# A conditional region between the halves of a product, and a last copy shared by two engines, in a routed attention and mixture-of-experts kernel

## The chip, the cores and the metric

The kernel runs on one core of one Trainium2 chip. The metric is the device time of one execution in microseconds (us), lower is better. The median of the runs of the kernel before is 705.09 us.

## The reference

The computation is an attention block with clusters, followed by a mixture of experts with one expert per token. What matters here is the second part, with 3072 tokens, 512 features, 8 experts and a hidden width of 1024:

```python
def _moe_ref(x, expert_emb, tau, w1, w2):
    N, D = x.shape
    ...
    logits = xn @ en.T / tau
    expert_idx = np.argmax(logits, axis=1)
    ...
    gate_w = probs[np.arange(N), expert_idx]
    out = np.zeros((N, D), dtype=np.float32)
    for e in range(E):
        mask = expert_idx == e
        if not mask.any():
            continue
        h = np.maximum(x[mask] @ w1[e], 0.0)
        out[mask] = gate_w[mask, None] * (h @ w2[e])
    return out.astype(np.float32)
```

How many tokens an expert gets depends on the data, so the kernel has to be right for every distribution.

## The kernel before

The attention fills about the first half of the time. Behind it the experts' work is a list of items, each for one expert: four early items, eight "sized" items (one per expert, with a fixed number of token slots from 272 down to 160), and eight "block" items of 128 tokens each for what the sized ones don't hold. The list `later` holds the last 16 of these, alternating: its numbers 13, 14 and 15 are a block, the sized item with 160 slots, and the last block. Two weight buffers `w1s` and `w2s` (slots 0 and 1) alternate; blocks 13 and 15 both use slot 1.

The order of the instructions is written out by hand for all engines (`manual_schedule`), so that each engine runs its instructions in the order in which the code issues them. A block goes as follows:

- DVE turns the gathered rows (`turn_x`, L1173).
- PE makes the first product in two halves (`hidden`, L1289); ACT applies the relu to each half into the tile `hT` (L1296).
- PE makes the second product (`result`, L1305): four matmuls that need the first half of `hT` and four that need the second, summed in one bank `y_ps`.
- ACT copies `y_ps` to `y`, scaled by the gate (L1316), and POOL scatters the rows of `y` to the output (L1080).

A sized item goes alike, with `sized_hidden` (L1204, relu at L1211; its results go through four banks in turn, three of `psH` and one of `psX`), `order_w2` (DVE reorders w2, L1189), `sized_result` (L1241, turned back by DVE at L1250 and scaled at L1264) and `send` (scatters, L1080). SP loads the weights (L1119).

If the fixed slots and blocks are not enough, the function `overflow` computes up to 14 further blocks of kind "whole". Its body stands under `tc.If(n_used > KX)` (L1565), where `n_used` is read from the tile `used` by every engine (L1550). With the inputs of the reference the body is not entered. Every engine that has work in the body still loads the register and branches, and on the path past the body it raises its semaphores by what the body would have raised, after waiting for its own work in front of the region (SP also for its weight loads, POOL also for the landing of its gathers and scatters). Work behind the region that depends on another engine waits for these raised values.

In the kernel before, `overflow()` stands at the head of the step for `later[14]`, in front of the weight loads of the last block:

```python
            if i == LAST - 1:
                overflow()
                weights1(later[LAST])
                weights2(later[LAST])
```

Of the kernel before, what the change touches and what calls it, by code (L numbers as in the profile page):

```python
# [9 lines left out]
F32 = mybir.dt.float32  # L10
BF16 = mybir.dt.bfloat16
I32 = mybir.dt.int32
ALU = mybir.AluOpType
ACTF = mybir.ActivationFunctionType
# [4 lines left out]
P = 128  # L19
# [20 lines left out]
def kernel(  # L40
# [12 lines left out]
    nc = tc.nc  # L53
# [3 lines left out]
    E, DM = moe_expert_emb.shape  # L57
    F = moe_w1.shape[2]
# [6 lines left out]
    KF = F // P  # L65
# [7 lines left out]
    CAPS = (272, 256, 240, 224, 208, 192, 176, 160)  # L73
    KX = 8
# [11 lines left out]
    scale = 1.0 / float(D) ** 0.5  # L86
# [80 lines left out]
    def bank(kind, pool):  # L167

        tiles = turns.setdefault(kind, [])
        if len(tiles) < 2:  # L170
            name = f"{kind}{len(tiles)}"
            tiles.append(pool.tile([P, 512], F32, tag=name, name=name))
            return tiles[-1]
        tiles.append(tiles.pop(0))
        return tiles[-1]
# [926 lines left out]
    def expert_of(it):  # L1102
        table = {"early": e_early, "sized": e_sized, "block": e_block, "whole": e_block}[it.kind]
        return nc.values_load(
            table[0:1, it.j : it.j + 1], engines=(EngineType.SP,), min_val=0, max_val=E - 1
        )
# [10 lines left out]
    def load_part(w, x, e, chunks, i, parts):  # L1117
        c = slice(chunks // parts * i, chunks // parts * (i + 1))
        nc.sync.dma_start(  # L1119
            out=w[:, c], in_=x[ds(e, 1)].rearrange("o (c p) f -> p (o c) f", p=P)[:, c]  # L1120
        )
# [108 lines left out]
    def sized_result(it):  # L1230

        d, C, n = mo[it], CAPS[it.j], WIDE[it.j]
        ys = d["ys"] = szp.tile([P, max(WIDE), P], F32, tag="ys", name="ys")
        cut = KF - 2
        bks = {}

        def products(g, fs):
            if g not in bks:
                bks[g] = misc() if g >= 2 else bank("y_ps", psY)
            for f in fs:  # L1240
                nc.tensor.matmul(  # L1241
                    bks[g][:, 0:C],
                    lhsT=d["w2"][:, f, P * g : P * g + P],
                    rhs=d["hT"][:, f, 0:C],
                    start=(f == 0),
                    stop=(f == KF - 1),
                )

        def turn_back(g):
            nc.vector.transpose(  # L1250
                ys[:, 0:n, SQ * g : SQ * g + SQ],
                bks[g][:, 0 : SQ * n].rearrange("p (u t) -> p u t", t=SQ),
            )

        products(0, range(cut))
        products(1, range(cut))
        for g in range(2):
            products(g, range(cut, KF))
            turn_back(g)
        for g in range(2, KD):  # L1260
            products(g, range(KF))
            turn_back(g)
        u0 = FIRST[it.j]
        nc.vector.tensor_tensor(  # L1264
            ys[:, 0:n], ys[:, 0:n], bc(flat(gates4)[:, u0 : u0 + n], [P, n, P], 2), ALU.mult
        )
# [9 lines left out]
    def flat(t):  # L1276
        return t.rearrange("p k w -> p (k w)")

    def hidden(it, halves=(0, 1)):

        d = mo[it]
        for half in halves:
            if half == 0:
                d["hT"] = mop.tile([P, F], F32, tag="hT", name="hT")
            f0 = 512 * half
            bk = psH.tile([P, 512], F32, tag="h_ps", name="h_ps")
            for m in range(0, 512, P):
                for c in range(KD):
                    nc.tensor.matmul(  # L1289
                        bk[:, m : m + P],  # L1290
                        lhsT=w1s[it.slot][:, c, f0 + m : f0 + m + P],
                        rhs=d["xT"][:, P * c : P * c + P],
                        start=(c == 0),
                        stop=(c == KD - 1),
                    )
            nc.scalar.activation(d["hT"][:, f0 : f0 + 512], bk, ACTF.Relu)  # L1296

    def result(it, halves=(0, 1)):
        d = mo[it]
        for half in halves:  # L1300
            if half == 0:
                d["y_ps"] = bank("y_ps", psY)
            bk = d["y_ps"]
            for c in range(KF // 2 * half, KF // 2 * half + KF // 2):
                nc.tensor.matmul(  # L1305
                    bk,
                    lhsT=d["hT"][:, P * c : P * c + P],
                    rhs=w2s[it.slot][:, c],
                    start=(c == 0),
                    stop=(c == KF - 1),  # L1310
                )
            if half == 1:
                to = (sidxs[0] if it.kind == "early" else it.tables[2])[:, it.col : it.col + 1]
                y = mop.tile([P, DM], F32, tag="y", name="y", bufs=3)
                gate = d["gate"] if it.kind == "early" else it.gates[:, it.col : it.col + 1]
                nc.scalar.activation(y, bk, ACTF.Copy, scale=gate)  # L1316
                scatter(out[:], to, y, N)
                del mo[it]

# [30 lines left out]
    later = items[KA:]  # L1350
# [73 lines left out]
    with tc.manual_schedule(engines=by_hand):  # L1424
# [123 lines left out]

        def overflow():
            n_used = nc.values_load(used[0:1, 0:1], min_val=0, max_val=KX + NO)  # L1550
            slot = later[-1].slot

            def more(j0, n):
                for j in range(j0, j0 + n):
                    it = Item("whole", KX + j, slot, more_tables)
                    it.col, it.gates, it.xin = j, more_gates, xin
                    weights1(it)
                    weights2(it)
                    fetch(it)
                    order_x(it)  # L1560
                    turn_x(it, nc.scalar.copy)
                    hidden(it)
                    result(it)

            with tc.If(n_used > KX):  # L1565
                more_tables = [None] + [
                    mop.tile([P, NO], I32, tag=f"more{i}", name=f"more{i}", bufs=1)
                    for i in range(2)
                ]
                xin = szp.tile([P, max(WIDE), P], F32, tag="ys", name="ys")[:, 0:NQ]  # L1570
                pb.hot_blocks(NB, NO)
                pb.tokens(NO)
                pb.token_rows(more_tables[1], more_tables[2])
                more_gates = mop.tile([P, NO], F32, tag="more_gates", name="more_gates", bufs=1)
                pb.hot_gates(NO)
                pb.gates(more_gates)
                more(0, MORE[0])
                with tc.If(n_used > KX + MORE[0]):
                    more(MORE[0], MORE[1])
                    with tc.If(n_used > KX + MORE[0] + MORE[1]):  # L1580
                        more(MORE[0] + MORE[1], MORE[2])

        LAST = len(later) - 1
        for i, it in enumerate(later):
            if i == LAST - 1:
                overflow()
                weights1(later[LAST])
                weights2(later[LAST])
            if it.kind == "sized":
                order_w2(it)  # L1590
            if i + 1 < len(later):
                turn_x(later[i + 1])
            if i > 0 and i + 2 < len(later) and later[i + 2].kind == "sized":
                fetch(later[i + 2])
            if i > 0 and later[i - 1].kind == "sized":
                send(later[i - 1])
                if i == LAST:
                    nc.gpsimd.drain()
            if it.kind == "sized":
                sized_hidden(it)  # L1600
            else:
                hidden(it)
            if i == 0:
                pb.gates(slot_gates)
            for j in range(i + 2, min(i + 4, len(later))):
                if later[j].kind == "block" and later[j] not in mo:
                    if it.kind == "sized":
                        nc.gpsimd.tensor_copy(pace, mo[it]["hT"][0:1, KF - 1, 0:1])
                        fetch(later[j])
            if i + 2 < LAST:  # L1610
                weights1(later[i + 2])
                if it.kind == "sized":
                    weights2(later[i + 2])
            if it.kind == "sized":
                sized_result(it)
            else:
                result(it)
            if i == 0:
                fetch(later[2])
                spread_gates()  # L1620
            if i + 2 < LAST and it.kind != "sized":
                weights2(later[i + 2])
# [45 lines left out]
```

## Time and profile before

| | |
|---|---|
| runs of the kernel before | 704.33, 706.35, 704.28, 705.85 us; median 705.09 |
| the profiled execution | 706.03 us, span from first to last instruction 704.2 us |
| granted TensorE clock | 0.999 |
| PE busy | 688.3 us (98% of the span) |
| DVE, ACT, POOL busy | 385.7, 262.8, 252.4 us |
| PE's last matmul starts / span ends | 697.9 / 704.2 us |

How to read what follows: times in a view are microseconds from the start of the span. PE is the matrix engine and PEld its weight loads, which overlap the matmuls; DVE, ACT and POOL are the vector, scalar and GpSimd engines; SP issues DMA. A name with a q (PEldq, ACTq) is the engine's instruction queue, with its branches and semaphore instructions, which are not counted as busy. An fp32 matmul leaves two records. Matmuls are pipelined, so that one record may last 0.59 us while the next starts 0.43 us after it; their ends are modelled. In brackets stands the idle time of an engine ahead of an instruction and what ended it; "remote" is a releaser that the trace does not name.

### The profile page before, as it was taken

How to read it: one execution, taken by the hardware profiler on the slowest of the kernel's cores; microseconds unless marked ns; L12 is line 12 of the kernel's file. 1: busy time of each engine (PE TensorE's matmuls, PEld its weight loads, DVE VectorE, ACT ScalarE, POOL GpSimd, SP SyncE). 2: the span in 40 equal slices, each digit the busy share in tenths (PEclk: the TensorE clock that was granted, in tenths of full speed). 3: DMA queues.
4: the chain of work that ended last, by engine and by line, in shares of the span. 5: the costliest groups of instructions: out<-in, count | busy, mean ns of one | idle time of the engine just before them, and what ended most of it. 6: DMA issues, size and time to landing. Idle time of an engine off the chain costs nothing.

```text
span 704.2 us, 16130 instructions
## 1 busy us (share of the span) xinstructions
PE 688.3 (98%) x6517; PEld 460.9 (65%) x6517; DVE 385.7 (55%) x666; ACT 262.8 (37%) x444; POOL 252.4 (36%) x403
## 2 busy tenths in 40 slices
PE   8999999999999999999999999999999999999896
PEld 3544444444444444455866678887979797979694
DVE  5878988998989999999573121240311203030210
ACT  5556565577656765576224110101010111111111
POOL 2122221321122221263215356646363554545402
PEclk9999999999999999999999999999999999999999
DMA  9765667785887578688799967358768585969360
GB/s 139 98 99 101 100 95 98 148 141 106 105 141 150 97 154 157 170 254 252 195 308 361 336 237 280 100 204 290 258 237 306 180 314 218 317 229 332 117 240 32
DMA packets 244156, 135.55 MB, mean 192 GB/s; under 512 B 207840, under 2 KB 207842, under 8 KB 244076
## 3 DMA queue, kind: packets, MB, share of 16 engines
q1 hardware_dynamic: 237084, 121.08, 65.4%
q0 software_dynamic: 6016, 13.12, 5.2%
q8 instruction: 54, 0.88, 0.5%
q10 hardware_dynamic: 976, 0.25, 0.2%
q14 instruction: 26, 0.21, 0.1%
HBM read 115.92 MB, written 13.12 MB: 183 GB/s over the span
## 4 chain that ended last, share of the span: by engine, by line
PE 75%; DVE 8%; issue 6%; DMA 6%; SPq 1%; ACT 1%; POOL 1%; another core or an unknown queue 1%; POOLq 0%; DVEq 0%; ACTq 0%
PE s_ps L512 16%; PE o_ps L534 12%; PE h_ps L1289 10%; PE y_ps L1305 9%; PE h_ps L1204 9%; PE misc L1241 5%; PE y_ps L1241 5%; DVE acc L553 4%; DMA out_dram<-ys,spidx 3%; PE x_ps L1204 3%; PE misc L581 2%; PE misc L405 1%; SPq L212 1%; DMA q<-in_q_dram 1%
## 5 line engine op out<-in xcount | busy, mean ns | idle before, releaser
L523 ACT ACTIVATE prob<-s_ps 128x768 f32<-128x768 f32 x192 | 154.2, 813 | 105.4 <-PE s_ps L512 104.4
L512 PE MATMUL s_ps<-qT,kT 64*64 64x384 f32 x1536 | 156.1, 482 | 0.0
L534 PE MATMUL o_ps<-prob,v 64*64 64x385 f32 x1536 | 142.1, 484 | 0.0
L553 DVE TENSOR_TENSOR acc<-acc,prob 128x768 f32<-128x768 f32 x128 | 127.3, 995 | 8.8 <-ACT prob L523 0.5
L534 PEld LDWEIGHTS o_ps<-prob,v 64*64 64x64 f32 x1536 | 59.3, 133 | 64.2 <-issue 56.3
L1250 DVE STREAM_TRANSPOSE ys<-y_ps 128x256 f32<-128x256 f32 (+4 forms) x16 | 6.5, 413 | 155.5 <-PE y_ps L1241 139.4
L1289 PE MATMUL h_ps<-xTm,w1s 128*128 128x128 f32 x768 | 88.8, 275 | 1.5 <-issue 1.5
L1289 PEld LDWEIGHTS h_ps<-xTm,w1s 128*128 128x128 f32 x768 | 87.5, 192 | 3.2 <-issue 2.8
L567 POOL TENSOR_TENSOR o_sum<-o_sb 128x385 f32<-128x385 f32 x30 | 29.9, 998 | 162.3 <-ACT o_sb L558 162.3
L1305 PE MATMUL y_ps<-w2s,hT 128*128 128x512 f32 x192 | 85.3, 594 | 1.7 <-ACT hT L1296 1.0
L1080 POOL DMA_INDIRECT out_dram<-ys,spidx x56 | 57.0, 1018 | 74.0 <-DVE ys L1264 59.4
L512 PEld LDWEIGHTS s_ps<-qT,kT 64*64 64x64 f32 x1536 | 56.1, 133 | 36.3 <-issue 32.2
L1296 ACT ACTIVATE hT<-h_ps 128x512 f32<-128x512 f32 x24 | 14.3, 596 | 163.0 <-PE h_ps L1289 119.0
L1204 PE MATMUL h_ps<-xTs,w1s 128*128 128x272 f32 (+7 forms) x384 | 72.9, 346 | 1.3 <-ACTq L1565 1.3
L1204 PEld LDWEIGHTS h_ps<-xTs,w1s 128*128 128x128 f32 x384 | 66.6, 190 | 8.1 <-issue 2.4
L512 PE MATMUL s_ps<-hot 64*64 64x384 bf16 x768 | 65.1, 325 | 1.9 <-ACT prob L523 0.7
L1305 PEld LDWEIGHTS y_ps<-w2s,hT 128*128 128x128 f32 x192 | 35.3, 190 | 42.9 <-issue 40.3
L1069 POOL DMA_INDIRECT xs<-x_rows,gpidx x56 | 56.4, 1008 | 17.1 <-issue 17.1
L512 PEld LDWEIGHTS <-hot 64*64 64x64 bf16 x768 | 24.3, 106 | 45.3 <-issue 41.9
L602 POOL COPY inv<-inv 32x12 f32<-32x12 f32 x120 | 31.2, 260 | 50.7 <-DVE inv L599 46.3
L1241 PE MATMUL misc<-hTs,w2o 128*128 128x272 f32 (+7 forms) x256 | 48.0, 346 | 0.0
L1241 PE MATMUL y_ps<-hTs,w2o 128*128 128x272 f32 (+7 forms) x256 | 48.0, 346 | 0.0
(270 smaller groups left out, 688.6 us busy)
## 6 DMA issues: line engine op xcount, KB each, us to landing
w1s<-in_moe_w_dram SPq DMA_DIRECT2D x18, 2048.0 KB
w2s<-in_moe_w_dram SPq DMA_DIRECT2D x18, 2048.0 KB
v<-in_v_dram SPq DMA_DIRECT2D x128, 48.0 KB
k<-in_k_dram SPq DMA_DIRECT2D x62, 96.0 KB
q<-in_q_dram SPq DMA_DIRECT2D x60, 96.0 KB
x_rows<-xb SPq DMA_DIRECT2D x60, 96.0 KB
xr<-x_rows SPq DMA_DIRECT2D x9, 512.0 KB
w1s<-in_moe_w_dram SPq DMA_DIRECT2D x4, 1024.0 KB
```

Source lines behind the costliest of these rows:

```text
L512: nc.tensor.matmul(s_ps[D * half : D * half + D, h, 0:HS], lhsT=l[rows, half], rhs=r[rows], start=part == (1 if len(parts) < 2 else 0), st ...
L523: nc.scalar.activation(d["prob"][:, :, 0:HS], d["s_ps"][:, :, 0:HS], ACTF.Exp, scale=scale)
L534: nc.tensor.matmul(g["o_ps"][D * h : D * h + D, half, 0:HE], lhsT=ld[n]["v"][keys, j, h], rhs=d["prob"][keys, h, 0:HE], start=(j == 0), st ...
L553: nc.vector.tensor_tensor(g["acc"], g["acc"], d["prob"][:, :, 0:HS], ALU.add)
L567: add(t["o_sum"][:, hq], t["o_sb"][:, 0], t["o_sb"][:, 1], ALU.add)
L602: nc.gpsimd.tensor_copy(inv2[M * to : M * to + M, :, i % 2], inv[M * i : M * i + M])
L1069: nc.gpsimd.indirect_dma_start(out=to, out_offset=None, in_=of, in_offset=bass.IndirectOffsetOnAxis(ap=at, axis=0), bounds_check=n - 1, oo ...
L1080: inst = nc.gpsimd.indirect_dma_start(out=to, out_offset=bass.IndirectOffsetOnAxis(ap=at, axis=0), in_=of, in_offset=None, bounds_check=n - 1,
L1204: nc.tensor.matmul(bk, lhsT=w1s[it.slot][:, c, P * f : P * f + P], rhs=d["xT"][:, c, 0:C], start=(c == 0), stop=(c == KD - 1),)
L1241: nc.tensor.matmul(bks[g][:, 0:C], lhsT=d["w2"][:, f, P * g : P * g + P], rhs=d["hT"][:, f, 0:C], start=(f == 0), stop=(f == KF - 1),)
L1289: nc.tensor.matmul(bk[:, m : m + P], lhsT=w1s[it.slot][:, c, f0 + m : f0 + m + P], rhs=d["xT"][:, P * c : P * c + P], start=(c == 0), stop ...
L1305: nc.tensor.matmul(bk, lhsT=d["hT"][:, P * c : P * c + P], rhs=w2s[it.slot][:, c], start=(c == 0), stop=(c == KF - 1),)
```

## The change

Two parts. First, `overflow()` moves in the code from the head of the step for `later[14]` to the middle of the second product of `later[13]`: behind the four matmuls of its first half and in front of the four of its second half, and so also in front of that block's copy of `y` and its scatter. For this the items of the region get other tiles: `hT` is taken from the sized items' tile `hTs`, `y_ps` from the pool `psH`, and their weights go to the slot of `later[13]`. At the end of the region's body the second half of that block's `w2` is loaded again. Second, for the last block alone the copy of `y_ps` to `y` is made by ACT for columns 0 to 255 and by DVE for columns 256 to 511.

```diff
@@ hidden @@
             if half == 0:
-                d["hT"] = mop.tile([P, F], F32, tag="hT", name="hT")
+                d["hT"] = (
+                    flat(szp.tile([P, KF, max(CAPS)], F32, tag="hTs", name="hTs", bufs=1))[:, 0:F]
+                    if it.kind == "whole"
+                    else mop.tile([P, F], F32, tag="hT", name="hT")
+                )
@@ result @@
             if half == 0:
-                d["y_ps"] = bank("y_ps", psY)
+                d["y_ps"] = (
+                    psH.tile([P, 512], F32, tag="h_ps", name="h_ps")
+                    if it.kind == "whole"
+                    else bank("y_ps", psY)
+                )
@@ result @@
                 gate = d["gate"] if it.kind == "early" else it.gates[:, it.col : it.col + 1]
-                nc.scalar.activation(y, bk, ACTF.Copy, scale=gate)
+                h = DM // 2 if it is later[-1] else DM
+                nc.scalar.activation(y[:, 0:h], bk[:, 0:h], ACTF.Copy, scale=gate)
+                if h < DM:
+                    nc.vector.tensor_scalar(y[:, h:DM], bk[:, h:DM], gate, None, ALU.mult)
                 scatter(out[:], to, y, N)
@@ overflow @@
-            slot = later[-1].slot
+            own = later[-3]
...
-                    it = Item("whole", KX + j, slot, more_tables)
+                    it = Item("whole", KX + j, own.slot, more_tables)
...
                     with tc.If(n_used > KX + MORE[0] + MORE[1]):
                         more(MORE[0] + MORE[1], MORE[2])
+                own.e = expert_of(own)
+                load_part(w2s[own.slot], moe_w2, own.e, KF, 1, 2)
@@ the loop over later @@
             if i == LAST - 1:
-                overflow()
                 weights1(later[LAST])
                 weights2(later[LAST])
...
             if it.kind == "sized":
                 sized_result(it)
+            elif i == LAST - 2:
+                result(it, (0,))
+                overflow()
+                result(it, (1,))
             else:
                 result(it)
```

## The prediction

> **What bounds the kernel now.** I read the page first: the share of PE, then the slices.
>
> ```profile
> PE 688.3 (98%) x6517; PEld 460.9 (65%) x6517; DVE 385.7 (55%) x666; ACT 262.8 (37%) x444; POOL 252.4 (36%) x403
> ```
>
> PE fills 98% of a span of 704.2 us, and the other engines have slack. So an edit is worth what it does to a gap of PE, or to the tail after PE's last instruction. Both edits lie in the last 50 us, so I went to the timeline of PE there.
>
> ```profile
> 650.67 7.31 PE L1289 MATMUL h_ps<-xTm,w1s 128*128 128x128 f32 x64
> 657.81 3.60 PE L1305 MATMUL y_ps<-w2s,hT 128*128 128x512 f32 x8
> 661.92 3.70 PE L1305 MATMUL y_ps<-w2s,hT 128*128 128x512 f32 x8 [0.51 <-ACT hT L1296]
> 666.89 3.50 PE L1204 MATMUL h_ps<-xTs,w1s 128*128 128x160 f32 x24 [1.27 <-ACTq L1565]
> ...
> 684.35 7.31 PE L1289 MATMUL h_ps<-xTm,w1s 128*128 128x128 f32 x64
> 691.49 7.03 PE L1305 MATMUL y_ps<-w2s,hT 128*128 128x512 f32 x16
> ```
>
> The columns are start, duration, engine and line, with the idle time before it and its releaser in brackets. The second product of the block before the last sized item is two pieces of 8 records (4 matmuls of two records each). Between them PE waits 0.51 us for the second half of hT. After them it waits 1.27 us for the conditional region at L1565. From 666.89 to 698.52 there is no further gap. So at most 1.8 us can be won in front of the last 32 us, and the rest is the tail. The timeline of ACT shows what else stands at these two places:
>
> ```profile
> 661.27 0.60 ACT L1296 ACTIVATE hT<-h_ps 128x512 f32<-128x512 f32 x1 [6.23 <-remote]
> 665.66 0.69 ACT L1316 ACTIVATE y<-y_ps,slot_gates 128x512 f32<-128x512 f32 x1 [3.79 <-PE y_ps L1305]
> ...
> 698.56 0.69 ACT L1316 ACTIVATE y<-y_ps,slot_gates 128x512 f32<-128x512 f32 x1 [4.68 <-PE y_ps L1305]
> ```
>
> Why the gap is 1.27 us is read from the region's own line:
>
> ```profile
> L1565 PEldq COMPARE_BRANCH  x1: 3837/3837/3837, 662.6 to 662.6; - x1
> L1565 ACTq COMPARE_BRANCH  x1: 45/45/45, 666.2 to 666.2; - x1
> L1565 PEldq EVENT_SEMAPHORE  x1: 51/51/51, 666.5 to 666.5; - x1
> L1565 ACTq EVENT_SEMAPHORE  x1: 17/17/17, 666.6 to 666.6; - x1
> L1565 POOLq COMPARE_BRANCH  x1: 45/45/45, 667.0 to 667.0; - x1
> L1565 POOLq INC_SWDGE_SEM  x1: 1230/1230/1230, 674.0 to 674.0; - x1
> ```
>
> PE's branch lasts 3.84 us, from 662.63 to 666.47, while its array works until 665.62; 0.85 us of it stick out. ACT branches only after its copy of y, and PE waits for the semaphore that ACT raises in the region (666.6). Both meet at 666.89.
>
> **The region (part one).** In the built program PE now issues 4 of the 8 matmuls, the region, then the other 4 and the sized item. Nothing is computed more or less when the region is not entered.
>
> PE's branch. PE's queue runs ahead of its array: the wait in front of y's first matmul was read at 655.8 and that matmul ran at 657.81, 2 us or 17 records later. The 8 records of the first half enter as slots come free, one per 0.11 us (7.31 us / 64), so the load of `used` is reached at about 656.8. Load to branch took 0.7 us (661.9 to 662.6), so the branch starts near 657.5 and ends near 661.3, at the duration of the row. The first half ends at 661.41. Then comes PE's wait on its own semaphore, one wait on weight queues (SP's part of the region ended at 656.9), and the matmul: in the trace the way from the branch's end to the matmul was 0.39 us with one wait more. That gives 661.8. The other condition, the second half of hT, comes at 661.87 as before ("remote" means that the trace does not name what released it, so I keep its time). I take a start of the second half at 662.0 in place of 661.92. Bounds: 661.45 if both are early (no gap at all); 662.65 if the branch can only finish once the array has drained, as it did 0.85 us after the drain in the trace (661.41 + 0.85 + 0.39).
>
> What follows. Eight records from 661.92 put the next one at 665.46 (the last of eight starts at 665.03, spacing 0.43), and the sized item started at 666.89. Now it stands directly behind, its ACT condition raised in the region: ACT branches after hT, not after y. ACT's load, branch and semaphore took 0.97 us from the start of the instruction before, so they are done at 662.25. The sized item starts at 662.0 + 3.54 = 665.54, **1.35 us earlier**; at the bounds 1.9 and 0.7 us. Its operands wait long: xTs was turned at 653.1 and w2o copied at 659.4.
>
> What is queued behind. ACT: y of this block now follows the region and also waits for the software-queue semaphores that POOL raises there; behind y stand the eight copies of hTs, and PE has four banks for them. POOL: its region now stands in front of this block's scatter, and waits for the scatters before it. The last of these six was made from 659.11 to 660.23; the DMA share falls to zero in the stretch after 661, so it landed about 661.5. Three semaphores (0.26 us) and the increment (1.23 us) follow: 663.0, 2.5 us before ACT needs it at 665.5. The scatter itself moves from 666.62 by at most a microsecond, and POOL had 18.45 us of idle before its next. SP: the load of the last block's w1s waits for PE's region, 666.5 in the trace and about 661.8 now; its w2s follows at 665.6 instead of 667.3. Both are used at 683 or later, so nothing changes. The additional reload of half of w2s lies inside the branch that is not taken. DVE's turn of xTm (666.68, released by ACT's region) goes to 662.3 and had 17 us of slack.
>
> **The last copy (part two).** One ACT copy of 512 columns (0.687 us) becomes ACT on 256 and DVE on 256. In the built program DVE does not wait for PE but for ACT's half, and POOL waits only for DVE. So they run one after the other. ACT with 256: the relu took 0.597 us on 512 and 0.30 on 160, 0.84 ns per column, so 0.687 - 0.213 = 0.47 us. DVE with 256 out of PSUM: turns of 128x256 took 0.44 us, a copy of 128x200 took 0.367; I take 0.42. The hop from ACT to DVE: 0.05 us (666.63 to 666.68). Sum 0.94 in place of 0.69: **0.25 us later**; bounds 0.4 later, and 0.2 earlier if both halves ran side by side. POOL's scatter follows 0.28 us after either engine, and the 0.97 us of the scatter and the end after it stay.
>
> The page PSUM — Partial Sum Buffer of the Trainium skill, in the section on PSUM bank collisions, says that two engines must not touch one bank and quadrant at once, readers included. That speaks against the halves, and would be why the program orders them; no run shown here has two readers in one bank. By that rule the sum is 0.25 us later; by the bare rows of the two halves side by side it would be 0.2 us earlier.
>
> The page Advanced Engine Details and Errata, section Control Flow Timing, gives about 108 ns for a compare-and-branch; the row on PE has 3837 ns. The page Runtime: NRT & Kernel Launch, section Instruction fetch mechanics, has a reason: a taken branch beyond the loaded window has to fetch its page first. By 108 ns the sum stays as it is and the first rival below goes; by the row the branch needs nearly all of the first half's 3.6 us.
>
> **Sum.** -1.35 + 0.25 = -1.1 us. The profiled execution took 706.03 us with a span of 704.2, so it becomes 704.9 with a span of 703.1. It stands at the slow end of its four runs (704.28 to 706.35); on their median of 705.09 it is **704.0 us**. A change under 0.3% (2.1 us) is about what a measurement of this kernel can't tell from none, and this lies under it. The bounds give -1.9 - 0.2 = -2.1 and -0.7 + 0.4 = -0.3.
>
> **Rivals.** *The branch is not covered (slower).* If PE loads `used` only when the first half has left the array (661.4), or its fetch queues behind another one, the 3.84 us stand bare: the branch ends at 661.41 + 0.7 + 3.84 = 665.9, the second half starts at 666.3, the sized item at 669.9, 3.0 us later than now, 3.2 with the tail: 708.3 us. Half of that exposed is +1.1 us, 706.2. It turns from gain to loss when the branch ends after about 662.7 (start of the second half 663.1, the sized item at 666.64, plus the tail's 0.25). For: the cover has only 0.1 us to spare. Against: the branches of ACT and POOL (45 ns) ran while their engines were busy, and PE's load came within 0.02 us of the first of four matmuls that were still to run. Chance 0.18.
>
> *POOL holds ACT (slower).* If POOL's region ends near 675.2, as it did before, ACT's y goes from 665.66 to 675.2, and hTs behind it to 676; PE fills its four banks until about 670 and then stands 6 us: 705.09 - 1.1 + 6 = 710. It decides from an end after about 669. Against: in the trace that region waited for the scatter issued at 666.62, and this one is no longer ahead of it. Chance 0.06.
>
> *Side by side.* Both halves of the copy overlap: -1.35 - 0.2 = -1.55 us, 703.5 us. Against: the order of waits in the program. Chance 0.08.
>
> **How the numbers follow.** The forecast has 0.68. Its four runs before spread over 2 us, so a true -1.1 reads as more than 2.1 us faster in about one of five (0.15 of it, with 0.05 from the side-by-side rival: 0.20). Slower by over 2.1 us: more than half of the uncovered branch (0.10) and POOL's hold (0.05): 0.15. The rest is 0.65. The range goes from -2.4 (the lower bound and a little spread), 702.7, to half of the uncovered branch with spread, 706.7; beyond it lie the fully bare branch and POOL's hold.
>
> **What would show it.** Right: a gap of 0.5 to 0.7 us between the two pieces of 8 records, none in front of L1204 behind them; PE's branch starting at 657 to 658; POOL's increment over by 663; at the end ACT's half, then DVE's, then the scatter, 0.94 us in all. Wrong: a gap over 1.7 us between the halves (the branch is bare), ACT's y later than 666 with PE idle in the sized item (POOL holds it), or a changed time with these stretches unchanged.

## The result and the profile after

The changed kernel takes 704.44 us (median), against 705.76 us for the kernel before on the same chip: a ratio of 0.9983, 95% interval 0.9977 to 0.9989, or 1.2 us faster; predicted were 704.0 us from 705.09, or 1.1 us faster. The profiled execution has a span of 702.5 us (704.2 before) at a granted clock of 0.999.

PE's timeline, to be held against the four lines of before around 657.81:

```profile
650.25 7.31 PE L1293 MATMUL h_ps<-xTm,w1s 128*128 128x128 f32 x64
657.40 3.60 PE L1313 MATMUL y_ps<-w2s,hT 128*128 128x512 f32 x8
661.53 3.70 PE L1313 MATMUL y_ps<-w2s,hT 128*128 128x512 f32 x8 [0.53 <-ACT hT L1300]
665.07 3.42 PE L1204 MATMUL h_ps<-xTs,w1s 128*128 128x160 f32 x24
...
689.60 7.03 PE L1313 MATMUL y_ps<-w2s,hT 128*128 128x512 f32 x16
```

The gap of 0.5 us between the halves, which ACT's `hT` releases, is still there. The gap of 1.27 us in front of the sized item (L1204) is gone. From the first matmul of the second product to the first of the sized item it was 666.89 - 657.81 = 9.08 us; now it is 665.07 - 657.40 = 7.67 us. I call this stretch *the stage*; it has shrunk by 1.41 us.

The region's own line (now L1576), as in the prediction:

```profile
L1576 PEldq COMPARE_BRANCH  x1: 3332/3332/3332, 656.9 to 656.9; - x1
L1576 PEldq EVENT_SEMAPHORE  x1: 51/51/51, 661.0 to 661.0; - x1
L1576 POOLq INC_SWDGE_SEM  x1: 1210/1210/1210, 661.4 to 661.4; - x1
...
L1576 ACTq EVENT_SEMAPHORE  x1: 17/17/17, 661.9 to 661.9; - x1
```

PE's branch runs from 656.90 to 660.23 and lies wholly beside the first half, which leaves the array at 661.00. PE's semaphore instruction (661.04) stands directly behind that end: it is PE's wait for its own work. What holds the second half after that is `hT`, from ACT's timeline:

```profile
660.88 0.60 ACT L1300 ACTIVATE hT<-h_ps 128x512 f32<-128x512 f32 x1 [6.26 <-remote]
```

It ends at 661.48 and the matmul starts at 661.53. At the end of the kernel the timeline of all engines shows the two halves of the copy and the scatter:

```profile
696.72 0.47 ACT L1325 ACTIVATE y<-y_ps,slot_gates 128x256 f32<-128x256 f32 x1 [4.73 <-PE y_ps L1313]
697.23 0.48 DVE L1327 TENSOR_SCALAR y<-y_ps,slot_gates 128x256 f32<-128x256 f32 x1 [13.36 <-ACT y L1325]
697.98 0.97 POOL L1080 DMA_INDIRECT out_dram<-y,sidx  x1 [7.78 <-DVE y L1327]
```

DVE waits for ACT, not for PE. PE's last product ends at 696.63, so 1.35 us pass until the scatter starts; before it was 699.53 - 698.52 = 1.01 us.

The account of the spans: the stage -1.41, from the sized item to PE's last end -0.07 (31.63 to 31.56), the tail behind PE +0.19 (5.68 to 5.87, the longer copy less a slightly shorter end). That is -1.29 us, and the medians differ by 1.32; single executions of either kernel scatter by some 5 us, so that two traces and two medians come this close is partly chance. The spans differ by 0.41 us more, because the first half of the second product starts 0.41 us earlier in this execution, ahead of the place that was changed.

### The profile page after: what moved, and what is told of

Read it like the earlier page. It is cut to its first block, busy times and chain, and to the rows that moved or that the text cites. A ratio compares the mean times of both kernels' runs of the same rounds, so it can differ in the third digit from the quotient of the medians.

```text
span 702.5 us, 16133 instructions
## 1 busy us (share of the span) xinstructions
PE 687.1 (98%) x6517; PEld 460.9 (66%) x6517; DVE 386.5 (55%) x667; ACT 262.8 (37%) x444; POOL 252.3 (36%) x403
## 4 chain that ended last, share of the span: by engine, by line
PE 76%; issue 8%; DVE 7%; DMA 3%; POOL 2%; ACT 1%; another core or an unknown queue 1%; SPq 0%; POOLq 0%; DVEq 0%; ACTq 0%
PE s_ps L512 16%; PE o_ps L534 13%; PE h_ps L1293 10%; PE y_ps L1313 9%; PE h_ps L1204 9%; PE misc L1241 5%; PE y_ps L1241 5%; PE x_ps L1204 3%; DVE acc L553 3%; PE misc L581 2%; DMA q<-in_q_dram 2%; PE misc L405 1%; DMA out_dram<-ys,spidx 1%; PE misc L660 1%
## 5 line engine op out<-in xcount | busy, mean ns | idle before, releaser
L1204 PE MATMUL h_ps<-xTs,w1s 128*128 128x272 f32 (+7 forms) x384 | 72.8, 346 | 0.0
L1204 PEld LDWEIGHTS h_ps<-xTs,w1s 128*128 128x128 f32 x384 | 66.7, 190 | 6.5 <-issue 2.9
```

Source lines behind the costliest of these rows:

```text
L1204: nc.tensor.matmul(bk, lhsT=w1s[it.slot][:, c, P * f : P * f + P], rhs=d["xT"][:, c, 0:C], start=(c == 0), stop=(c == KD - 1),)
```

## Experiments

Theory before these runs: the region costs PE time only through the gap around it, the move takes that gap from 1.27 us to almost nothing, and the halved copy gives a quarter of it back. The rival is that PE's branch of 3.3 to 3.8 us is what the place decides about, and that the new place only just covers it.

The kernels ran in three sets, each on one chip of its own with runs of the kernel before beside it (701.33, 703.59 and 706.06 us). The stage, measured in every trace:

| kernel (set) | stage, us | gap between the halves + gap in front of the sized item |
|---|---|---|
| before | 9.08 | 0.51 + 1.27 |
| after | 7.67 | 0.53 + 0 |
| old place, halved copy (1) | 8.11 | 0 + 1.08 |
| new place, one copy (1) | 7.41 | 0.30 + 0 |
| new place, two banks, ACT and DVE (1) | 7.41 | 0.30 + 0 |
| no region (1) | 6.87 | 0 + 0 |
| the change again (2) | 7.52 | 0.38 + 0 |
| old place, short body (2) | 7.33 | 0 + 0.30 |
| region in front of the product (2) | 10.00 | 0 + 0, and 3.52 in front of the product |
| new place, two banks, ACT (2) | 7.49 | 0.37 + 0 |
| old place, tiles of its own (3) | 8.83 | 0.45 + 1.08 |
| new place, shared bank (3) | 8.09 | 0.95 + 0 |
| region in front of the copy (3) | 8.73 | 0.54 + 0.90 |
| region in front of the copy, two banks, ACT (3) | 9.01 | 0.53 + 1.18 |

**The parts alone.** The region at its new place with one ACT copy at the end:

```diff
-                h = DM // 2 if it is later[-1] else DM
-                nc.scalar.activation(y[:, 0:h], bk[:, 0:h], ACTF.Copy, scale=gate)
-                if h < DM:
-                    nc.vector.tensor_scalar(y[:, h:DM], bk[:, h:DM], gate, None, ALU.mult)
+                nc.scalar.activation(y, bk, ACTF.Copy, scale=gate)
```

> The region in its new place with its own tiles; the last block's result copied by ACT alone, as in the kernel before. Theory (the place gives the gain, the halved copy costs): the gap in front of L1204 goes from 1.27 us to 0, the sized item follows its predecessor 1.43 us sooner; from PE's last matmul to the end of y 0.72 us, as before; 1.4 us faster than before (ratio 0.9980) and 0.36 us faster than the change as made. Rival (the halved copy carries part of the gain): slower than the change as made, 0.9 us or less faster than before.

And the halved copy in the kernel before:

```diff
-                nc.scalar.activation(y, bk, ACTF.Copy, scale=gate)
+                h = DM // 2 if it is later[-1] else DM
+                nc.scalar.activation(y[:, 0:h], bk[:, 0:h], ACTF.Copy, scale=gate)
+                if h < DM:
+                    nc.vector.tensor_scalar(y[:, h:DM], bk[:, h:DM], gate, None, ALU.mult)
```

> The region in its old place; only the last block's copy in two halves. Theory: ACT's half 0.47 us, then DVE's half 0.48 us, 1.08 us from PE's last matmul to the end of y instead of 0.72; the gap of 1.27 us stays; 0.36 us slower than before (ratio 1.0005). Rival (halves help): 0.2 us or more faster.

Measured: the region alone 0.9993 (0.9984 to 1.0002), 0.5 us faster; the halves alone 1.0005 (0.9996 to 1.0014), 0.35 us slower, with 1.31 us from PE's end to the scatter. Neither interval leaves out 1. The region brought less than the stage of the first two traces says, and PE's timeline of the region alone shows why:

```profile
654.13 3.60 PE L1313 MATMUL y_ps<-w2s,hT 128*128 128x512 f32 x8
658.03 3.67 PE L1313 MATMUL y_ps<-w2s,hT 128*128 128x512 f32 x8 [0.30 <-PEq L1573]
661.54 3.42 PE L1204 MATMUL h_ps<-xTs,w1s 128*128 128x160 f32 x24
```

```profile
L1573 PEldq COMPARE_BRANCH  x1: 3712/3712/3712, 653.6 to 653.6; - x1
L1573 PEldq EVENT_SEMAPHORE  x1: 51/51/51, 657.8 to 657.8; - x1
```

```profile
654.33 0.60 ACT L1300 ACTIVATE hT<-h_ps 128x512 f32<-128x512 f32 x1 [2.98 <-PE h_ps L1293]
```

Here the second half is not released by `hT` but by PE's own queue in the region, after 0.30 us. PE's branch was over at 657.34, still under the first half, which left the array at 657.73; only then does PE's wait for its own work end. ACT's relu followed the first product at once in all four traces of this set; in the traces of before and after it started over 3 us later than that. With `hT` on time the old place has no gap between the halves, and in front of the sized item (timeline, then the region's line, of the halves alone):

```profile
662.18 3.53 PE L1204 MATMUL h_ps<-xTs,w1s 128*128 128x160 f32 x24 [1.08 <-ACTq L1568]
```

```profile
L1568 PEldq COMPARE_BRANCH  x1: 3388/3388/3388, 655.5 to 655.5; - x1
L1568 PEldq EVENT_SEMAPHORE  x1: 51/51/51, 661.1 to 661.1; - x1
L1568 ACTq COMPARE_BRANCH  x1: 45/45/45, 661.7 to 661.7; - x1
L1568 ACTq EVENT_SEMAPHORE  x1: 17/17/17, 662.1 to 662.1; - x1
```

PE's branch was over at 658.9, 2.2 us before the product left the array. ACT came last: it branches only behind its copy of `y`. So on this chip the old place costs 1.08 us through ACT, the new one 0.30 us through PE's wait for an empty array, and the move gains 0.70 us of stage, not 1.41. The move alone was not run on a chip with a late `hT`.

**No region at all**, one copy at the end (the overflow blocks are left out of the computation):

```diff
                 result(it, (0,))
-                overflow()
                 result(it, (1,))
```

> As the region alone, but without the call of the region (the overflow blocks, which these inputs do not use, are left out). Theory (the moved region costs nothing any more): the gap between the halves of the second product stays at 0.5 us, since it is hT's, and there is none behind; same time as the region alone within 0.2 us. Rival (the branch is what holds the second half): the gap between the halves shrinks to 0.1 us or less, 0.4 us faster than the region alone.

Measured: 0.9966 (0.9952 to 0.998), 2.4 us faster than before. Its stage is 0.54 us shorter than with the region at the new place, and the gap between the halves is gone:

```profile
653.69 7.03 PE L1313 MATMUL y_ps<-w2s,hT 128*128 128x512 f32 x16
660.56 3.42 PE L1204 MATMUL h_ps<-xTs,w1s 128*128 128x160 f32 x24
```

So the expectation's theory, that the moved region costs nothing, is wrong where `hT` is on time. The rival's size fits, but not its reason: the region holds the second half by PE's wait for its empty array, when the branch is already over. A further 0.67 us comes from the end: the scatter's start to the end of the span takes 3.88 us in place of 4.55, and SP goes through 6 final semaphores there in place of 10. Against the region alone that accounts for 1.2 of 1.9 us (0.9966 against 0.9993); the stage also starts 0.44 us earlier in this trace, which nothing here explains. So with `hT` on time a better place could give at most 0.54 us of stage.

**Where the price of PE's branch comes from.** The region in front of the whole second product:

```diff
-                result(it, (0,))
-                overflow()
-                result(it, (1,))
+                overflow()
+                result(it)
...
-                load_part(w2s[own.slot], moe_w2, own.e, KF, 1, 2)
+                weights2(own)
```

> The region moved alone (one ACT copy at the end), but to the place between the first and the second product of the same block, in front of all 16 matmuls of the second product. Theory 'length': PE's taken branch lasts 3.3 to 3.8 us whatever the array does, starting about 1.4 us before the first product leaves the array, because PE's queue reads some 17 short matmuls ahead; so it ends 1.9 to 2.4 us after that, 0.3 us of semaphores follow, and the gap between the two products is 2.2 to 2.7 us with none later: 1.1 to 1.6 us slower than the kernel before where that one has a gap of 1.08 us in front of the sized item, 0.4 to 0.9 us slower where it has 0.5 + 1.27 us. Rival 'drain': the branch itself costs little (45 ns as on ACT) and only lasts until the array is empty; then the gap is 0.3 us and the kernel 0.8 us faster than before.

Measured: 1.0056 (1.004 to 1.0071), 3.9 us slower. The direction is that of "length" and against "drain", but the size was missed. PE's timeline, the stretches around it (the column behind the busy times is the granted clock), and the branch:

```profile
659.20 10.16 PE L1313 MATMUL y_ps<-w2s,hT 128*128 128x512 f32 x16 [3.52 <-PEq L1573]
669.20 3.42 PE L1204 MATMUL h_ps<-xTs,w1s 128*128 128x160 f32 x24
```

```profile
655.70:659.20 3.50, 0.00 (x1) 0.03 (x1) 0.78 (x3) 0.37 (x1) 1.93 (x2) 0.90 0.17 50
659.20:664.00 4.80, 4.80 (x6) 2.15 (x7) 0.71 (x1) 0.23 (x1) 0.00 (x0) 0.50 0.84 282
```

```profile
L1573 PEldq COMPARE_BRANCH  x1: 3452/3452/3452, 654.1 to 654.1; - x1
L1573 PEldq EVENT_SEMAPHORE  x1: 51/51/51, 658.8 to 658.8; - x1
```

```profile
658.83 0.60 ACT L1300 ACTIVATE hT<-h_ps 128x512 f32<-128x512 f32 x1 [6.10 <-remote]
```

The branch ends at 657.6, 1.9 us after the first product left the array at 655.67, as foreseen. Two things were not. PE's own wait in the region ended only at 658.83, together with ACT's late relu, so the gap is 3.52 us. And the granted clock fell to 0.50, near 658.5 and so still inside the gap, and stayed there for the first seven of the product's sixteen records (two to a matmul), which stand 0.85 us apart in place of 0.43: 10.16 us in place of 7.03. The gap cost its length and 3.1 us more.

The record has two more long gaps of PE. They stand near 400 us in the two kernels further down with the region in front of the copy, where PE waits for `w2s`, 2.54 us in the one and 3.53 us in the other. Both times the product behind took 8.80 us, and 7.11 in the trace of before. In the first of them (the second view is of the stretches before, in and after the slow part):

```profile
402.36 8.80 PE L1313 MATMUL y_ps<-w2s,hT 128*128 128x512 f32 x16 [2.54 <-DMA w2s<-in_moe_w_dram]
```

```profile
402.30:403.30 1.00, 0.94 (x3) 0.49 (x4) 0.00 (x0) 0.00 (x0) 0.00 (x0) 1.00 1.06 412
403.40:406.70 3.30, 3.30 (x6) 1.24 (x5) 0.00 (x0) 0.00 (x0) 0.00 (x0) 0.50 1.06 398
406.80:411.00 4.20, 4.20 (x11) 1.62 (x9) 0.00 (x0) 0.00 (x0) 0.00 (x0) 1.00 1.03 411
```

The clock fell 1 us after the matmuls had begun again. No gap of 1.27 us or less lowered it in any trace. The Trainium skill, TensorE: Matmul & The Clock Gate, section "What's actually happening", says that an idle window of about 3.4 us sends the array back to half its clock. The gap of 3.52 us would fit that; the one of 2.54 us is shorter and did it too, so by the measurement less idle time is enough.

The other test of the price is the kernel before with a short body, so that the jump is near; it also takes ACT's semaphore out of the region:

```diff
-                more(0, MORE[0])
-                with tc.If(n_used > KX + MORE[0]):
-                    more(MORE[0], MORE[1])
-                    with tc.If(n_used > KX + MORE[0] + MORE[1]):
-                        more(MORE[0] + MORE[1], MORE[2])
```

> The kernel before with the region at its old place, but without the overflow blocks in its body (it then computes nothing for a seventh and further block of a crowded expert list; with these inputs the region is not entered). ACT has nothing left in the region and neither branches nor raises a semaphore; PE's and DVE's parts stay, with a shorter jump. Theory 'ACT's turn': the old gap in front of the sized item is ACT's, which loads, branches and signals only after its copy of y; without it the gap falls from about 1.1 to 0.3-0.4 us (PE's own wait until its array is empty, and its semaphores), 0.7 us faster than before or more. Rival 'PE's branch': PE's branch sticks out; its row stays at 3.3 us or more, ends after the array, and the gap stays near 1.1 us. If the jump's distance makes the price, the row falls under 1 us.

Measured: 0.9981 (0.9972 to 0.999), 1.3 us faster at the old place. The region's line and PE's timeline:

```profile
L1565 PEldq COMPARE_BRANCH  x1: 236/236/236, 659.3 to 659.3; - x1
```

```profile
663.51 3.50 PE L1204 MATMUL h_ps<-xTs,w1s 128*128 128x160 f32 x24 [0.30 <-PEq L1565]
```

PE's branch takes 0.24 us in place of 3.3 to 3.8. The size of the body that is jumped over sets the price here, and the array's state does not. The Trainium skill, Runtime: NRT & Kernel Launch, section Instruction fetch mechanics, says that a taken branch to a target outside the loaded window has to fetch that page first; this pair of rows agrees. In the stretch of each of the twelve long branches the DMA view has one packet on the instruction queue q8, and in that of the short one none. The kernel does two things at once, though: PE's long branch and its wait for ACT are both gone, so it does not tell which of them made the old gap. (ACT still branches here, against the expectation, but only at 663.78, when the sized item has started.)

**Which of the two made the old gap.** The region between the whole second product (16 records) and the copy of its result: PE meets it at the old place, ACT one copy earlier.

```diff
-                result(it, (0,))
-                overflow()
-                result(it, (1,))
+                result(it, (0, 1))     # the matmuls
+                overflow()
+                result(it, (2,))       # the copy and the scatter
```

> Region between all 16 matmuls of the second product and the copy of their result (one ACT copy at the end). PE meets it at the old place, its jump as far as before; ACT meets it before its copy of y in place of behind it. Theory 'ACT's turn': ACT's branch and signal are long over when the product ends, PE's branch of 3.3 to 3.8 us lies under the product where that is not held up, and what is left is PE's own wait for its empty array: a gap of 0.3 us in front of the sized item, 7.33 us from the product's first matmul to the sized item's (7.41 to 7.52 with the region between the halves): 0.8 us faster than before, 0.1 to 0.2 us faster than the region between the halves. Rival 'PE's branch': PE meets the region where it did, so the gap stays at 1.1 us or more.

This kernel also loses the copies and scatters of the first two early blocks, which ask for their halves by number, and near 400 us it has the gap of 2.54 us and the slow product shown above. So its total (1.0009, 0.9994 to 1.0024) can't be read; the stage can. PE's timeline and the region's line:

```profile
663.20 3.70 PE L1313 MATMUL y_ps<-w2s,hT 128*128 128x512 f32 x8 [0.54 <-ACT hT L1300]
667.79 3.50 PE L1204 MATMUL h_ps<-xTs,w1s 128*128 128x160 f32 x24 [0.90 <-ACT y L1324]
```

```profile
L1573 ACTq EVENT_SEMAPHORE  x1: 17/17/17, 663.5 to 663.5; - x1
L1573 PEldq COMPARE_BRANCH  x1: 3568/3568/3568, 663.8 to 663.8; - x1
```

ACT's turn can't be the whole of it. ACT had signalled at 663.56, yet the gap is 0.90 us: PE's branch lasted until 667.37, while the product left the array at 666.90. (The view names ACT's copy of `y`, which ended 0.12 us ahead of the matmul; the last kernel of this section, with the same place and a branch 0.28 us longer, has a gap 0.28 us longer and names PE's queue.) On this chip `hT` was late again (a gap of 0.54 us between the halves), and that is the link. While the second half waits for `hT`, PE's queue stands at that wait and can't read ahead to the region: here the branch starts 0.66 us after the relu's end, and 0.66 to 0.76 us after it in all five traces with the region behind a late `hT`, while with `hT` on time (the halves alone) it started 1.5 us after the product's first matmul. The late branch then outlasts the half's 3.7 us. So the old place has two limits close together. With `hT` on time, PE reads ahead and ACT's turn remains (1.08). With `hT` late, the branch sticks out as well (0.85 us in the trace of before, 0.90 of gap here without ACT). The new place avoids both, since the queue meets no wait on `hT`'s second half in front of the region.

The trace of before can now be read more closely than its view does. Where ACT comes last (the halves alone, and the tiles alone below), the sized item starts 0.05 us behind ACT's semaphore. Where PE's branch comes last (here and in the last kernel of this section), it starts 0.31 us behind PE's. In the trace of before it started 0.24 us behind ACT's (666.65) and 0.31 us behind PE's (666.58). The view names ACT, but by these distances PE's branch ended that gap of 1.27 us; ACT's turn alone would have ended it 0.2 us sooner, at the same 1.08 us.

**The tiles.** The kernel before with the other tiles for the region's items alone (the first two hunks of the change):

> The kernel before with the tiles of its own alone, the region at its old place. Theory: no change (within 0.3 us), and the gap of 1.1 us or more in front of the sized item is still there, released by ACT's region. Rival: the tiles loosen PE's wait in front of the sized item; then the gap falls to 0.3-0.4 us, as in the kernel with the short region, 0.7 us faster.

Measured: 1.0003 (0.9988 to 1.0019), with 0.45 + 1.08 us of gaps and the branch from 663.16 to 666.77:

```profile
667.33 3.53 PE L1204 MATMUL h_ps<-xTs,w1s 128*128 128x160 f32 x24 [1.08 <-ACTq L1573]
```

The tiles alone bring nothing that the runs show. And the new place without the other bank, with one ACT copy at the end:

```diff
-                d["y_ps"] = (
-                    psH.tile([P, 512], F32, tag="h_ps", name="h_ps")
-                    if it.kind == "whole"
-                    else bank("y_ps", psY)
-                )
+                d["y_ps"] = bank("y_ps", psY)
```

> The region at the new place, one ACT copy at the end, but the second product's result in the shared pair of banks as before the change, not in a tile of its own; the tile of its own for hT stays. PE's second half of the product then waits until ACT has raised its semaphore in the region, not only for hT. Theory: ACT needs 0.97 us from the start of hT's second half to that semaphore in place of 0.6, so the gap between the halves is 0.4 us longer where the second half of hT is late (0.8 in place of 0.38), and unchanged (0.30) where it is on time. Rival: the tile of its own does nothing for time, and the gap is the same in both cases.

Here it is the region's items that lose their bank. Measured: 0.9987 (0.9972 to 1.0002), and PE's timeline:

```profile
662.36 3.70 PE L1309 MATMUL y_ps<-w2s,hT 128*128 128x512 f32 x8 [0.95 <-ACTq L1569]
```

`hT` was late in this trace too. The gap is 0.95 us against 0.53 in after: 0.42 us, as expected. The tiles belong to the move: with a shared bank the second half has to wait for ACT to leave the region.

**The last copy.** The last product in two banks of 384 and 128 columns, the region at the new place; ACT copies the first while PE works on the second, DVE copies the second:

```diff
+        cuts = ((0, 384), (384, DM))
+        bks = [bank("y_ps", psY) for _ in cuts]
...
+        nc.scalar.activation(y[:, 0:384], bks[0][:, 0:384], ACTF.Copy, scale=gate)
+        nc.vector.tensor_scalar(y[:, 384:DM], bks[1][:, 0:128], gate, None, ALU.mult)
```

> The region as in the change; the last block's second product goes to two banks, columns 0 to 383 and 384 to 511, each half of the sum first into the one, then into the other; ACT copies the first bank while PE still works on the second, DVE copies the second. Theory (the halves are serial because they share a bank, so two banks free them): DVE starts within 0.05 us of PE's end and takes 0.35 us, 0.4 us from PE's end to the end of y instead of 1.08 with the halves and 0.72 with ACT alone; PE's product takes as long as before, 7.0 us; 1.75 us faster than before (ratio 0.9975). Rival (the writes of one tile y order them, not the bank): DVE still starts after ACT, but ACT is early; then the same time. Rival (the additional matmuls cost): PE's product takes 7.5 us and the gain is eaten.

Measured: 0.999 (0.9981 to 0.9999), 0.7 us faster where 1.75 were expected, and not to be told from the region alone. From the timeline:

```profile
691.92 0.58 ACT L1320 ACTIVATE y<-y_ps,slot_gates 128x384 f32<-128x384 f32 x1 [5.51 <-PE y_ps L1310]
692.76 0.35 DVE L1321 TENSOR_SCALAR y<-y_ps,slot_gates 128x128 f32<-128x128 f32 x1 [12.88 <-PE y_ps L1310]
693.89 0.97 POOL L1080 DMA_INDIRECT out_dram<-y,sidx  x1 [7.65 <-DVE y L1321]
```

DVE now waits for PE. ACT had ended 0.26 us before DVE started, so the trace alone would not tell, but in the built program DVE has no wait for ACT left: the order of the halves did come from the shared bank. All of `y` is ready 0.39 us after PE's end (692.72). But the scatter starts 0.78 us after DVE in place of 0.28; in POOL's queue a separate semaphore instruction, which waits for DVE and ended at 693.15, stands in front of it, and the scatter itself waits for ACT. With both copies on ACT:

```diff
-        nc.vector.tensor_scalar(y[:, 384:DM], bks[1][:, 0:128], gate, None, ALU.mult)
+        nc.scalar.activation(y[:, 384:DM], bks[1][:, 0:128], ACTF.Copy, scale=gate)
```

> Region at the new place; the last block's second product goes into two banks, 384 and 128 columns, and ACT copies both, the first while PE still works on the second. The scatter then waits for ACT alone. Theory: 0.58 us of copy in the shadow of PE, then about 0.05 + 0.28 us, and the scatter 0.28 us later: PE's end to the scatter's start 0.65 us in place of 1.05 (one ACT copy) and 1.35 (the halves); PE pays 0.08 us for the cut. 0.3 us faster than the region moved alone. Rival: the scatter needs an extra wait here too (0.78 us after the copy as with two engines), then nothing is gained.

```profile
694.86 0.58 ACT L1320 ACTIVATE y<-y_ps,slot_gates 128x384 f32<-128x384 f32 x1 [4.07 <-PE y_ps L1310]
695.70 0.37 ACT L1321 ACTIVATE y<-y_ps,slot_gates 128x128 f32<-128x128 f32 x1 [0.26 <-PE y_ps L1310]
696.34 0.97 POOL L1080 DMA_INDIRECT out_dram<-y,sidx  x1 [7.17 <-ACT y L1321]
```

Measured: 0.9969 (0.9957 to 0.9981), a median of 701.45 us. From PE's end (695.66) to the scatter it takes 0.68 us, as expected. The change itself ran beside it:

> The whole change once more, beside the others on one chip. Sum of the parts as measured alone: region -0.7 (if the second half of hT is on time) to -1.4 us (if it is late and covers the wait), halves +0.2 to +0.36 us: 0.3 to 1.1 us faster than before, ratio 0.9985 to 0.9996. It also shows whether the second half of hT is late here (a gap of 0.5 us between the halves that ACT releases) or on time (0.3 us, PE's own wait).

Measured: 0.9982 (0.9973 to 0.9991), a median of 702.22 us: slightly more gain than expected, since the kernel before, of which there is no trace on this chip, can be assumed to have had its late `hT` (here the relu started 3.4 us after the last record of its half). From PE's end to the scatter it takes 1.36 us here. So the two banks on ACT are 0.7 us better at this point, pay 0.08 us in PE (7.11 for 7.03 us), and beat the kernel before. Against the change the medians differ by 0.77, but the two intervals overlap and there are six runs of the one and eleven of the other, so that gain is not shown in the total.

The region in front of the copy was also combined with the two banks:

> The same place of the region, and the last product in two banks of 384 and 128 columns, both copied by ACT. Theory: the sum of both, 0.8 + 0.4 = 1.2 us or more faster than before (ratio 0.998 or below), and faster than the change by 0.5 us. Rival: as with the region in its old place, 0.4 us faster than before only.

It too lacks the two early blocks' copies and has the gap of 3.53 us near 400 us, and its total (1.0002, 0.9988 to 1.0015) can't be read. PE's timeline has the gap in front of the sized item, with a branch of 3.85 us that ends at 668.69:

```profile
669.11 3.50 PE L1204 MATMUL h_ps<-xTs,w1s 128*128 128x160 f32 x24 [1.18 <-PEq L1596]
```

The hope for a shorter stage fell with that of the kernel above. Its tail repeats the 0.68 us.

## Why the prediction was right, and where it was not

- **The move.** Predicted -1.35 us, measured -1.41 in the stage. The parts held relative to the first half's start: the second half 4.19 us later was predicted and 4.13 measured, the sized item 7.73 and 7.67.
- **PE's branch.** It was to start near 657.5 and end at 661.3, with 0.1 us of cover to spare. It started at 656.90 and ended at 660.23, with 0.8 us to spare: measured from the start of the first half it came 0.2 us earlier than my estimate (-0.5 for -0.3), and this branch took 3.33 us, not 3.84. The cover held in every trace of the new place, by 0.3 to 0.8 us.
- **What made the old gap.** The prediction had PE and ACT "both meet at 666.89". The later kernels say that PE's branch was last there, by 0.2 us. The way from the branch's end to the matmul was 0.42 us there, not 0.39. The sum did not depend on either, since the move takes both engines out of the way.
- **POOL and ACT.** The increment was to be over by 663.0 and was at 662.6; ACT's region was to be done at 662.25 and was at 661.9. POOL held nobody.
- **The halved copy.** Predicted +0.25 us, measured +0.34 from PE's end to the scatter and 0.35 as the difference in the total of the halves alone. The term that was too small is DVE's half: 0.48 us, not 0.42; ACT also started 0.05 us later behind PE. "Side by side" did not happen, and the two banks showed that one shared bank was the reason.
- **What the prediction took over without a price.** It kept the time of `hT` as a given. That gap of 0.5 us is no property of the kernel: on another chip it was absent, and then the same move was worth 0.70 us of stage and, with the halves, about 0.15 us in sum (-0.5 + 0.35, neither distinguishable from nothing). The forecast of -1.1 us fits the chips on which `hT` is late, and named no such condition; that the result was measured where `hT` is late was partly luck.
- **The first rival was too cheap.** It priced a fully bare branch, with the array empty for 4.9 us, at 3.0 us. The three long gaps of PE cost 1.7, 1.7 and 3.1 us on top of their length, because the granted clock fell. By an estimate from these, that rival's time should have stood some 2 to 3 us higher.

## What to carry to other kernels

Put a conditional region that is rarely entered where each engine's queue can read ahead to it, with enough matmuls issued in front of it and no wait on another engine just before it. Look at each engine's part by itself, because removing one limit (ACT's turn) only uncovered the next (PE's branch). Splitting this copy over two engines gained nothing while both read one bank; split the product over two banks, let the larger piece be copied in the shadow of the matmuls, and keep the last pieces on one engine, so that what follows waits for one semaphore.

## What the runs showed of the hardware

- PE's branch over the long body took 3.33 to 3.85 us in twelve traces, whatever the array did; over the short body it took 0.24 us. ACT's, POOL's and DVE's branches took 45 to 72 ns over the same long body.
- Gaps of 2.54, 3.52 and 3.53 us on PE brought the granted clock to 0.50, and the product behind them took 8.80, 10.16 and 8.80 us in place of 7.03 to 7.11. Gaps up to 1.27 us did not.
- From about 375 us on, in the traces of the result and of sets 2 and 3, ACT's relu of the second half of a block's first product started 0.9 to 3.8 us after the start of that product's last matmul record, but for one product near 400 us (0.3 us in every trace) and one product each in the two kernels that lack early copies (6.7 and 8.8 us). In the traces of set 1 it was 0.3 us for every product. The kernel before took 701.33 us on that chip and 703.59 to 706.06 us in the other measurements. In the trace with the region in front, PE's wait for its own work ended together with this late relu, so it is PE's signal that is late. What delays it, and why not on every chip, stays open.
